# Lightning attention and a leaky-ReLU block: halves of the features, attention output on chip, compact state, weight combinations on GpSimd, TensorE in text order

## The chip, the cores and the metric

One core of a Trainium2 chip; the sets of runs used different chips. The metric is the device time of one execution in microseconds, as the median of the timed runs. A profiled execution gives the span (first to last instruction), 1.7 to 1.8 us less than its timed figure. Words used below: a *hole* is time in which TensorE waits; a *bank* is one buffer of the kernel's PSUM pool, into which its matmuls write, and tiles with the same tag share banks; a *clean* duration is that of an instruction that no other engine's work lengthens, for VectorE the mean of those that no GpSimd work overlaps; *blocking* is what VectorE's instructions took beyond that, a measured excess and not a mechanism.

## The reference, cut to what matters

```python
# q, k, v: (4, 8, 768, 64); lam: 8 decays near 0.98; blocks of 64 positions
intra = einsum('bhic,bhjc->bhij', qb, kb) * Dmask          # decayed, causal
out   = einsum('bhij,bhjd->bhid', intra, vb) + einsum('bhid,bhde->bhie', qb * lam_pow, kv_state)
kv_state = lam_block * kv_state + einsum('bhsd,bhse->bhde', kb * rev_pow, vb)
# x = out as 3072 tokens x 512
h = x @ w_in                       # 512 -> 2048, weights arrive as float64
y = maximum(0.01 * h, h) @ w_out   # 2048 -> 512
```

## The kernel before

Attention runs in chunks of 128 tokens (24 chunks, 25 pipelined *steps*: step s transposes chunk s and finishes chunk s-1). The two matrix products run in 12 *groups* of 256 tokens, each as seven products of combined quarters instead of eight (*up* to 2048 features in two calls, then one *down*). The combinations of quarters are tensor additions on VectorE. The float64 weights are turned into float32 on chip: 32 *blocks*, four VectorE operations each, then three subtractions for every pair of blocks.

```python
# weights, after the four conversion operations of a block
def t13(): nc.vector.tensor_tensor(w[:, 4:6, :], w[:, i + 1:i + 3, :], w[:, i:i + 2, :], op=ALU.subtract)
def t2():  nc.vector.tensor_tensor(at(s["T2"]), at(s["B22"]), at(s["T1"]), op=ALU.subtract)
def t4():  nc.vector.tensor_tensor(at(s["T4"]), at(s["B21"]), at(s["T2"]), op=ALU.subtract)

# one step, in text order (a = chunk to transpose, b = the chunk before it)
ps = scores of b (two PSUM banks, tag "ps")        # 64 rows, paired
sc = ps * decay                                    # VectorE, "the masks"
load(a + 2); kT[a] = transposed(k, bank "pt")      # TensorE, copied out by ScalarE
po  = state[b-1] x qsT[b]                          # state 128x128, half of it zeros
qT[a] = transposed(q, bank "pt"); qsT = qT * pow_q # GpSimd
pu  = k[b] x v[b] (tag "ps"); state = lam * state + pu   # GpSimd, VectorE, two halves
po += sc x v; xc = copy(po); dma(xs[b] <- xc)      # the attention output goes to DRAM
# ... cut ...
attend(7); need(FO // 2); load_x(0); up(0, 0)      # load_x reads xs back
attend(5); need(FO); up(0, 1)
attend(11); load_x(1); need(2 * FO); down(0)
for g in range(1, NG):
    up(g, 0); attend(1); up(g, 1)
    if g + 1 < NG: load_x(g + 1)
    down(g)
```

Every engine's order is set by a scheduler that takes what is ready, the earlier in the text first. It works before the run; in the traces of the change, e1 and e13, which share their start, every engine runs the start's instructions in the same order.

## Time and profile before

| | before |
|---|---|
| median of the timed runs | 776.83 us (773.8 to 777.11; 776.74 with a fourth run) |
| span of the profiled run | 773.9 us |
| TensorE busy | 729.7 us (94%) |
| VectorE, ScalarE, GpSimd busy | 299.8, 198.4, 73.2 us |
| moved by DMA | 55.33 MB |
| last weight conversion ends | 209.7 us |
| down of group 0 ends | 225.6 us |

The 94% tells little here: the share is an average over a start of about 220 us, in which TensorE has holes, and a long full part in which it has none.

### The profile page before, as it was taken

What the parts mean: (1) busy time and instruction counts of PE and PEld (TensorE: products, weight loads), DVE (VectorE), ACT (ScalarE), POOL (GpSimd) and SP (SyncE); (2) the same over time, 40 slices, a digit from 0 to 9 for tenths busy, and PEclk for the clock granted to TensorE, in tenths of its full rate; (3) what the DMA queues carried; (4) which work ended last, traced back from release to release, by engine and by line L of the source; (5) the groups of instructions that cost most, each with busy time, mean ns of one, the idle gap of its engine ahead of it and who ended that gap; (6) DMA issues with size and microseconds to landing.
All of it is one profiled execution on the core that took longest, in us unless ns stands there. A gap on an engine that the chain in (4) does not pass through costs nothing.

```text
span 773.9 us, 12415 instructions
## 1 busy us (share of the span) xinstructions
PE 729.7 (94%) x5312; PEld 672.6 (87%) x5312; DVE 299.8 (39%) x530; ACT 198.4 (26%) x353; POOL 73.2 (9%) x81
## 2 busy tenths in 40 slices
PE   4587999888999999999999999999999999999998
PEld 3476988777899899899998999989999899998997
DVE  6965799986613223023141230412303223032130
ACT  3423735433213022031130311302213022131220
POOL 2333141624300000000000000000000000000000
PEclk9889999999999999999999999999999999999999
DMA  9979795976400001000000000000000000000000
GB/s 227 268 183 260 193 258 130 225 190 158 118 28 19 24 28 42 14 15 28 28 29 14 15 28 28 26 3 28 28 28 2 28 28 28 28 1 28 28 1 28
DMA packets 96198, 55.33 MB, mean 71 GB/s; under 512 B 76688, under 2 KB 84880, under 8 KB 96144
## 3 DMA queue, kind: packets, MB, share of 16 engines
q1 hardware_dynamic: 96000, 54.54, 26.5%
q8 instruction: 42, 0.69, 0.4%
q14 instruction: 12, 0.10, 0.0%
q10 hardware_dynamic: 144, 0.00, 0.0%
HBM read 41.95 MB, written 12.58 MB: 70 GB/s over the span
## 4 chain that ended last, share of the span: by engine, by line
PE 83%; DVE 10%; issue 3%; ACT 2%; POOL 1%; DMA 1%; SPq 0%; ACTq 0%; DVEq 0%; POOLq 0%
PE Z L426 21%; PE Z L407 20%; PE W L426 11%; PE W L407 10%; PE Y L426 5%; PE Y L407 5%; PE ps L283 3%; PE pt L270 2%; PE po L326 2%; PE pu L310 2%; PE po L299 2%; DVE sc L287 1%; DVE wo L202 1%; DVE wo L206 1%; DVE state L319 1%
## 5 line engine op out<-in xcount | busy, mean ns | idle before, releaser
L407 PE MATMUL Z<-x,wi 128*128 128x128 f32 x1536 | 186.7, 275 | 1.0 <-ACT tmp L363 1.0
L407 PEld LDWEIGHTS Z<-x,wi 128*128 128x128 f32 x1536 | 179.5, 192 | 2.4 <-ACT tmp L363 1.2
L407 PE MATMUL W<-x,wi 128*128 128x128 f32 x768 | 93.9, 275 | 0.0
L407 PEld LDWEIGHTS W<-x,wi 128*128 128x128 f32 x768 | 89.8, 192 | 0.0
L426 PE MATMUL Z<-wo,gA 128*128 128x256 f32 x384 | 88.0, 380 | 0.0
L426 PE MATMUL W<-wo,gS 128*128 128x256 f32 x384 | 87.2, 379 | 0.0
L426 PE MATMUL Z<-wo,gS 128*128 128x256 f32 x384 | 86.9, 379 | 0.0
L426 PEld LDWEIGHTS W<-wo,gS 128*128 128x128 f32 x384 | 72.9, 190 | 10.0 <-issue 0.2
L426 PEld LDWEIGHTS Z<-wo,gS 128*128 128x128 f32 x384 | 72.8, 190 | 9.8
L426 PEld LDWEIGHTS Z<-wo,gA 128*128 128x128 f32 x384 | 71.6, 190 | 9.4 <-DVE wo L206 0.2
L363 ACT COPY tmp<-Z 128x512 f32<-128x512 f32 (+1 forms) x72 | 37.0, 514 | 156.2 <-PE Z L426 108.5
L395 ACT ACTIVATE gA<-gA 128x512 f32<-128x512 f32 x72 | 45.4, 630 | 111.9 <-DVE gA L372 45.3
L383 DVE TENSOR_TENSOR gA<-tmp,Z 128x512 f32<-128x512 f32 x24 | 16.5, 687 | 103.2 <-PE Z L407 103.2
L383 DVE TENSOR_TENSOR os<-tmp,Z 128x256 f32<-128x256 f32 x12 | 5.1, 421 | 114.2 <-PE Z L426 114.2
L372 DVE TENSOR_TENSOR gA<-tmp,Y 128x512 f32<-128x512 f32 x24 | 16.5, 688 | 80.3 <-PE Y L407 80.2
L407 PE MATMUL Y<-x,wi 128*128 128x128 f32 x384 | 47.5, 276 | 0.0
L407 PEld LDWEIGHTS Y<-x,wi 128*128 128x128 f32 x384 | 45.2, 192 | 0.4 <-issue 0.2
L283 PE MATMUL ps<-qT,kT 64*128 64x128 f32 x384 | 37.8, 300 | 7.7 <-ACT qT L272 4.6
L426 PE MATMUL Y<-wo,gA 128*128 128x256 f32 x192 | 44.4, 379 | 0.0
L283 PEld LDWEIGHTS ps<-qT,kT 64*128 64x128 f32 x384 | 31.5, 198 | 14.3 <-ACT qT L272 7.1
L426 PEld LDWEIGHTS Y<-wo,gA 128*128 128x128 f32 x192 | 36.2, 190 | 4.8
L287 DVE TENSOR_TENSOR sc<-ps,decay 128x512 f32<-128x512 f32 x48 | 31.2, 686 | 22.2 <-PE ps L283 11.2
(66 smaller groups left out, 645.1 us busy)
## 6 DMA issues: line engine op xcount, KB each, us to landing
k<-in_k_dram SPq DMA_DIRECT2D x24, 256.0 KB, 4.8
q<-in_q_dram SPq DMA_DIRECT2D x24, 256.0 KB, 5.4
v<-in_v_dram SPq DMA_DIRECT2D x24, 256.0 KB, 5.8
ws<-in_moe_w_in_dram SPq DMA_DIRECT2D x12, 512.0 KB, 5.3
xs<-xc SPq DMA_DIRECT2D x24, 256.0 KB, 2.6
x<-xs SPq DMA_DIRECT2D x24, 256.0 KB, 2.9
out_dram<-os SPq DMA_DIRECT2D x24, 256.0 KB, 2.0
ws<-in_moe_w_out_dram SPq DMA_DIRECT2D x9, 512.0 KB, 4.0
```

The costliest lines, as they stand in the source:

```text
L270: nc.tensor.transpose(out=pt[:, hp, :], in_=pair(src, hp), identity=ident)
L283: nc.tensor.matmul(ps[hi][:, hp, :], lhsT=kT[b][HALF[hi], hp, :], rhs=qT[b][HALF[hi], hp, :], start=(hp == 0), stop=True, skip_group_check ...
L287: nc.vector.tensor_tensor(sc[:, hi], ps[hi], decay[:, hi], op=ALU.mult)
L299: nc.tensor.matmul(po[:, hp, :], lhsT=state[(b - 1) % 2][:, hp, :], rhs=qsT[b][:, hp, :], start=(hp == 0), stop=False, skip_group_check=True)
L310: nc.tensor.matmul(pu[:, hp, :], lhsT=pair(loaded[b][0], hp), rhs=pair(loaded[b][2], hp), start=(hp == 0), stop=True, skip_group_check=True)
L326: nc.tensor.matmul(po[HALF[hi], hp, :], lhsT=tv[:, 2 * hp + hi, :], rhs=sc[:, hi, hp, :], start=(not inter and hp == 0), stop=True, skip_g ...
L363: nc.scalar.copy(t[:, 0:cols], src)
L372: nc.vector.tensor_tensor(c11[0], s1, Y, op=ALU.add)
L383: nc.vector.tensor_tensor(c22[0], p5, Z, op=ALU.add)
L395: nc.scalar.activation(out=dst, in_=src, func=AF.Prelu, bias=0.0, scale=1.0, alpha=0.01)
L407: nc.tensor.matmul(t[:, i * C:(i + 1) * C], lhsT=w[:, kk, :], rhs=x[:, A[sa], kk, :], start=(first and i == 0 and kk == 0), stop=(i == UP ...
L426: nc.tensor.matmul(t, lhsT=G[g][sa][:, p, :], rhs=WO[p][:, SO[sb], :], start=(first and p == 0), stop=(p == NP - 1), skip_group_check=True)
```

## The change

Its intent is to reach the full part sooner. Only 13 of the 25 steps run before group 1; the other 12 are put between an up and a down of groups 1 to 6. Up and down are done by halves of the 2048 features, so the first half can start with half of the weights. The attention output stays in SBUF. The state keeps only its two useful halves. The subtractions of weights go to GpSimd. And TensorE's order is taken from the text. The core of the diff:

```diff
+    ctx.enter_context(tc.manual_schedule(engines={mybir.EngineType.PE}))
-    state = [const.tile([P, HP, P], F32, name=f"state{i}") for i in range(2)]
+    state = [const.tile([P, HP, D], F32, name=f"state{i}") for i in range(2)]
-                nc.vector.tensor_tensor(w[:, 4:6, :], w[:, i + 1:i + 3, :], w[:, i:i + 2, :], op=ALU.subtract)
+                nc.gpsimd.tensor_tensor(W[p][:, 4:6, :], W[p][:, i + 1:i + 3, :], W[p][:, i:i + 2, :], op=ALU.subtract)
 # ... T2 and T4 likewise; cut ...
+                load(a + 1)                       # was a + 2; q has 2 buffers instead of 3
-            qT[a] = transposed(loaded[a][1], "qT")
+            qT[a] = transposed(loaded[a][1], "qT", "ps", 2)
-            xc = xp.tile([P, KO * C], F32, name="xc", tag="xc")
-            nc.sync.dma_start(out=xs[b // 2, b % 2], in_=xc)
+            nc.scalar.copy(out=X[g][:, 2 * h:2 * h + 2].rearrange("p a k c -> p (a k) c"), in_=po)
 # ... state read and update as 64-wide tiles; product() adds the first half's result; cut ...
-    W_RATE = 0.7
+    W_RATE = 0.85
+    attend(5); need(NW // 4);     up(0, 0)
+    attend(3); need(NW // 2);     down(0, 0)
+    attend(3); need(3 * NW // 4); up(0, 1)
+    attend(2); need(NW);          down(0, 1)
     for g in range(1, NG):
+        for u in range(NU):
+            up(g, u)
+            attend(1)
+            down(g, u)
```

## The prediction

The old kernel's trace: item 1 is about VectorE's conversions, item 2 about a two-input elementwise operation on GpSimd (the scaling of k and of q), item 3 about matmuls (scores that start in pairs 7 ns apart, and the next start after a change of tile shape). The forecast's sum, 765 us of span and 768 us timed, is whole: the 14 us of blocking in it rest on 0.34 us per us of GpSimd, from that trace. That the rate would hold in the changed kernel was the author's estimate. So were the pairing of 64x64 tiles, the 0.06 us of a pair of 64 columns (about half of the 112 ns measured for 128 columns) and the factor 0.93 for overlapping instructions (two masks of 0.69 us each took 1.29 us together).

> **What bounds the kernel now.** I read the page's 40 slices first, then a table of windows, the chain of waits, the groups by shape, and single steps in the timeline.
>
> ```profile
> PE   4587999888999999999999999999999999999998
> ...
> DVE  6965799986613223023141230412303223032130
> ...
> DMA  9979795976400001000000000000000000000000
> ```
>
> There are two kernels in one. From slice 11 on (about 220 us) TensorE is full and everything else idles. Before that VectorE and the DMA engines are full and TensorE has holes. The windows put numbers on it (columns: stretch, length, busy time and count on PE, PEld, DVE, ACT, POOL, granted clock, DMA share, GB/s):
>
> ```profile
> 0.00:50.00 50.00, 28.58 (x207) 23.88 (x208) 38.35 (x78) 19.00 (x32) 14.88 (x23) 0.86 0.95 231
> 50.00:79.00 29.00, 23.27 (x243) 19.43 (x242) 14.04 (x27) 8.05 (x15) 10.34 (x11) 1.00 0.96 237
> 79.00:130.00 51.00, 48.34 (x426) 44.31 (x428) 47.14 (x86) 30.41 (x53) 12.60 (x13) 1.00 0.79 197
> 130.00:202.00 72.00, 61.49 (x573) 52.97 (x570) 58.59 (x94) 25.75 (x45) 32.57 (x32) 0.98 0.74 186
> ...
> 303.60:352.80 49.20, 49.20 (x338) 46.31 (x337) 12.08 (x21) 9.98 (x18) 0.00 (x0) 1.00 0.06 22
> ```
>
> The last line is one whole group of 256 tokens in the steady part: 49.2 us, all TensorE. Instruction starts are 112 ns apart in the up products and 216 ns in the down products, so 14 x 16 x 0.112 + 7 x 16 x 0.216 = 49.3. Twelve groups are 590 us and none of the change alters them. An attention step, from the same start-to-start intervals: scores 16 x 0.056 = 0.9 (two row halves start 7 ns apart, so a pair costs 112), transposes 8 x 0.11 = 0.9, state read 8 x 0.112 = 0.9, state update 0.9, output 16 x 0.055 = 0.9, and about 0.1 at each change of tile mode: 4.8 us. With 24 chunks, four of them without the state read and four without the update, that is 108 us. 590 + 108 = 698, so about 76 of 773.9 us is TensorE waiting or running slow, nearly all of it before 227 us, when group 1 begins. That is all the change can win.
>
> [...]
> 1. [...] The conversion's last step takes 685 ns where no GpSimd work overlaps it and 1094 ns where some does; the score mask, with one input in PSUM, keeps 685 either way. From 80 to 200 us GpSimd worked 43 us and the conversions cost 14.5 us more than their clean durations: 0.34 us of VectorE lost per us of GpSimd.
> 2. [...] The trace: 1127 and 1304 ns against 687 on VectorE for 128x512.
> 3. [...] The trace shows the paired starts and 202 to 205 ns instead of 112 at each change.
>
> **The change, part by part.**
>
> *Compact state.* The state read becomes 16 instructions of 64x64. If the diagonal tiles pair as the row halves do, it stays 8 x 0.112 = 0.9 us. The update becomes 16 instructions of 64 columns, 8 pairs at perhaps 0.06: 0.5 instead of 0.9. VectorE does one 0.42 us operation instead of two, GpSimd one 0.62 instead of two. A step falls to about 4.4 us of TensorE: 20 x 0.4 = 8 us, floor 690.
>
> *Output kept on chip.* 6.3 MB written and 6.3 MB read back go away. Together with fewer chunks up front, this lowers what the start must load: 14 chunks and all weights, 11.0 + 16.8 = 27.8 MB instead of 42.7 MB in the first 210 us.
>
> *Halves, and steps spread out.* Before, 23 of 25 steps ran before the first down; now 13, and 12 run inside groups 1 to 6. Only 13 x 4.4 + 49 = 106 us of TensorE work stands before group 1, so a long start becomes shorter, and the moved steps return later at full price: 12 x 4.4, about 52 us less the 6 that two late steps cost already.
>
> *Weight combinations to GpSimd.* 16 x (683 + 417 + 416) = 24 us of clean VectorE time leaves; GpSimd gains 16 x (1.27 + 2 x 0.62) = 40 us, of which 0.34 x 40 = 14 us comes back as VectorE blocking. Net gain about 10 us.
>
> *The new start, S.* Stage A, five steps and eight weight blocks: DMA-bound. The old kernel had moved six chunks and twelve blocks by 50 us at 95% DMA share; the new one needs six chunks and about as many blocks, since its stages load ahead: 48 us. The rest up to group 1: TensorE needs 8 steps and group 0. A step has its own latency, visible in the old kernel when VectorE was half idle:
>
> ```profile
> 59.80 1.29 DVE L287 TENSOR_TENSOR sc<-ps,decay 128x512 f32<-128x512 f32 x2 [3.58 <-PE po L326]
> ...
> 65.80 1.29 DVE L287 TENSOR_TENSOR sc<-ps,decay 128x512 f32<-128x512 f32 x2 [1.17 <-PE po L326]
> ...
> 71.19 1.29 DVE L287 TENSOR_TENSOR sc<-ps,decay 128x512 f32<-128x512 f32 x2 [2.56 <-PE po L326]
> ```
>
> That is 5.4 to 6 us from mask to mask. 8 x 6.2 + 49 = 99 us by that chain. VectorE over the same stretch: 24 blocks x 2.21 = 53, 8 masks and states 14, up adds and combinations 11, down adds 1: 79 clean, times 0.93 because consecutive starts overlap, 74; GpSimd works 30 on weights and 24 on steps, x 0.34 = 18; 92 plus 5% holes = 97, then the last half down of 12: 109. The two chains overlap imperfectly. S = 48 + 106 = 154, against 227.
>
> *Steady part.* Eleven groups x 49.2 = 541. In text order a step between up and down must wait for its masks, and VectorE first finishes the combination of the up just ended. The old kernel shows this very order (the 12 matmuls of another product fill TensorE here):
>
> ```profile
> 286.60 1.16 PE L283 MATMUL ps<-qT,kT 64*128 64x128 f32 x16
> ...
> 287.33 0.69 DVE L342 TENSOR_TENSOR gS<-gS,gA 128x512 f32<-128x512 f32 x1 [1.73 <-ACT gS L395]
> ...
> 288.06 0.69 DVE L343 TENSOR_TENSOR gS<-gS,gA 128x512 f32<-128x512 f32 x1
> ...
> 288.67 0.68 DVE L344 TENSOR_TENSOR gS<-gA,gS 128x512 f32<-128x512 f32 x1
> 288.69 1.50 PE L407 MATMUL Z<-x,wi 128*128 128x128 f32 x12
> 289.27 0.69 DVE L345 TENSOR_TENSOR gS<-gA,gS 128x512 f32<-128x512 f32 x1
> 289.87 1.28 DVE L287 TENSOR_TENSOR sc<-ps,decay 128x512 f32<-128x512 f32 x2
> ```
>
> Masks end 3.9 and 4.6 us after the scores begin. The q transposes and the state update now use the two score banks, so they follow at 4.0 and 4.65, the output at 5.3, and the step ends at 6.3 instead of 4.4. Nothing may fill the hole. If the masks go first, 4.5. I take 5.4 as the middle: 12 x 5.4 = 65, where a full stall gives 75 and none 54. In the second half down, VectorE adds the first half's result to the first product; in groups 7 to 11, with no step between, it follows the four combinations, free at 3.8 us where the third product wants the bank at 3.46: 5 x 0.4 = 2. Tail 3.4 as now.
>
> Sum: 154 + 541 + 65 + 2 + 3.4 = 765; the timed runs are about 2.5 above the span (776.83 against 773.9), so 768 us, 1.1% less than before. Of 73 us taken from the start, some 59 come back as steps inside the groups, nearly a fifth of them as holes.
>
> **Rivals.**
> - *The holes outweigh the start.* Every late step stalls in full (75), and GpSimd, 60 to 80% busy in the start, slows VectorE by 0.5 instead of 0.34: S = 163, total 787, over 1% slower. For it: the order shown above, and strict order takes away what fills holes today. Against: VectorE's busy digits are 2 to 3 in the steady part.
> - *No stalls and a tight start.* Masks are served before combinations (54) and S = 142, close to what 109 us of transfers (the packets' own time on 16 engines, 55 for 14 chunks and 54 for weights) and TensorE's 106 allow: 745, 4% faster. For it: the new rates and split points look tuned, and DMA stalls behind the store and reload vanish.
> - *The transfer was hidden anyway.* After 80 us the DMA share is 0.74 to 0.79, so the roundtrip matters only in stage A, where just 0.5 MB of it moved by 50 us. Keeping x on chip alone would then gain almost nothing; the gain is in which steps come early.
> - *64x64 tiles do not pair.* The state read costs 1.8 instead of 0.9: 20 x 0.9 = 18 us more, 786.
>
> **Range and chances.** S has a spread of about 8 us, the late steps of 8, pairing and the rest of 5: together some 12. The tuned look of the split points draws the low side out. 769, with 749 to 788 for 8 in 10. Faster by over 2% means under 761.3: 0.33. Slower means over 792.4: 0.06. Within: 0.61.
>
> **What would show it.** Group 1 begins near 154 us; a half up and half down keep 25 us together; a late step takes 4.5 (no stall) or 6.3 (stall), with the q transposes waiting for the mask; VectorE 95% busy from 50 to 140 us; conversions that overlap GpSimd over 1 us; the 64x64 pairs 7 ns apart. A start beyond 165, state reads at 1.8 us, or new holes in each half down would prove me wrong upwards; a start under 140 or masks served at once, downwards.

## The result, and the profile after

The changed kernel is correct and slower: 795.78 us median (795.26 to 799.42) against 776.74, ratio 1.0264, 95% interval 1.0224 to 1.0303. Ratios here are the mean time of one kernel's fast runs over that of the other's in the same rounds, so they are not quite the ratio of the medians quoted. The prediction was 769 with 749 to 788: the kernel is slower than the whole range.

The page of the changed kernel, for the slices shown before:

```profile
PE   5287879898999999998999999989999999999998
...
DVE  6969998623313323223143043132242322423223
...
POOL 3554677301101000001011010000000000000000
PEclk9688999999999999999999999999999999999999
DMA  9955766401021022011021000000000000000000
```

Both of the old saturated resources let go earlier: VectorE after slice 7 (the last conversion ends at 155.1 us) instead of slice 10 (209.7 us). The start did become shorter. TensorE's row hardly shows what was lost in return: an 8 in slices 9, 18 and 26 (counted from 0) among nines, because 9 stands for anything from 90% up, and 20 us in 624 are 3%. The windows (columns as in the prediction; cut at the first up, the last weight conversion, the end of group 0 and the last matmul):

```profile
0.00:53.40 53.40, 27.97 (x280) 22.91 (x280) 43.33 (x70) 19.48 (x33) 25.58 (x31) 0.81 0.97 251
53.40:155.10 101.70, 82.44 (x815) 72.21 (x814) 90.33 (x132) 50.29 (x88) 56.72 (x51) 0.92 0.60 153
166.30:790.50 624.20, 603.66 (x4489) 557.49 (x4487) 182.79 (x338) 129.78 (x232) 29.80 (x27) 0.99 0.08 21
```

The full part is 624.2 us long and TensorE's busy time is 20.5 us less. Who it waited for, from the view of waits (TensorE's rows: total us, times, longest), first in the full part alone (166.3 us to the end), then in the whole run:

```profile
PE pt L253 <- DVE sc L270: 17.5, 11, 3.1
PE po L311 <- DVE sc L270: 2.0, 2, 1.8
PE Z L416 <- DVE tmp L342: 1.1, 5, 0.2
```

```profile
PE pt L253 <- DVE sc L270: 35.2, 18, 5.5
PE pt L253 <- DMA k<-in_k_dram: 12.7, 2, 7.6
PE ps L266 <- DVE state L304: 5.6, 1, 5.6
PE ps L266 <- ACT qT L255: 4.4, 2, 3.6
PE po L277 <- POOL qsT L291: 2.1, 1, 2.1
```

In the full part 19.5 of 20.6 us are waits for a mask (L270), nearly all by the transposes of q (L253). The other half of the 35.2 us, and the waits for k, the state, qT and qsT, lie in the start. The timeline of one late step shows how:

```profile
212.05 1.16 PE L266 MATMUL ps<-qT,kT 64*128 64x128 f32 x16
...
212.78 0.69 DVE L327 TENSOR_TENSOR gS<-gS,gA 128x512 f32<-128x512 f32 x1 [0.27 <-ACT gS L376]
...
214.16 0.66 PE L253 MATMUL pt<-ident,k 128*128 128x128 f32 x4
214.72 0.68 DVE L330 TENSOR_TENSOR gS<-gA,gS 128x512 f32<-128x512 f32 x1
...
215.32 1.28 DVE L270 TENSOR_TENSOR sc<-ps,decay 128x512 f32<-128x512 f32 x2
216.06 0.66 PE L253 MATMUL pt<-ident,q 128*128 128x128 f32 x4 [1.24 <-DVE sc L270]
```

The scores are there at 213.2, but the masks start at 215.32, after the four combinations of the up just ended (L327 to L330). The q transposes want the bank that the first mask reads (the change gave them tag "ps"), and in text order nothing else may run. From up to down this step takes 6.10 us. Steps that begin a batch have no state read to fill the time; their hole is longer, and then this happens:

```profile
180.97 1.55 DVE L329 TENSOR_TENSOR gS<-gA,gS 128x512 f32<-128x512 f32 x1
...
183.77 1.12 PE L253 MATMUL pt<-ident,q 128*128 128x128 f32 x4 [3.13 <-DVE sc L270]
```

Four transposes took 1.12 instead of 0.66 us: after a hole of 3.13 us TensorE ran at half clock. The windows show the granted clock (0.50, third figure from the end), here and once more after the last late step, where the hole before was 1.83 us and the first product of the half down took 3.40 us:

```profile
183.45:186.86 3.41, 3.09 (x32) 2.76 (x34) 1.29 (x3) 0.59 (x1) 1.22 (x1) 0.50 0.22 52
528.20:531.60 3.40, 3.40 (x13) 2.51 (x10) 0.00 (x0) 0.59 (x1) 0.00 (x0) 0.50 0.03 5
```

Whether a hole of some length decides it is not shown. (L329 took 1.55 us while GpSimd was scaling k beside it, and 0.68 us where no GpSimd work overlapped it.) The two steps of this kind take 8.36 and 8.46 us. In e3 (below) the first of them had the same hole and kept its full clock:

```profile
179.98 0.66 PE L253 MATMUL pt<-ident,q 128*128 128x128 f32 x4 [3.12 <-DVE sc L270]
```

That step took 7.01 us. So the longer hole costs 0.9 us over the usual 6.10, and the half clock some 1.4 more.

From the starts of the matmuls, stage by stage, the sum of the prediction against the run:

| term | predicted, us | measured, us |
|---|---|---|
| start, until group 1 begins | 154 | 166.3 |
| twelve late steps | 65 | 77.1 |
| groups 1 to 11 | 541 + 2 | 547.1 |
| tail (3.8 in the old kernel, counted alike) | 3.4 | 3.8 |
| span | 765 | 794.3 |

### The profile page after: what moved, and what is told of

Same layout as the page of the kernel before. It is cut to its first block, busy times and chain, and to the rows that moved or that the text cites. A ratio compares the mean times of both kernels' runs of the same rounds, so it can differ in the third digit from the quotient of the medians.

```text
span 794.3 us, 12974 instructions
## 1 busy us (share of the span) xinstructions
PE 725.6 (91%) x5632; PEld 662.5 (83%) x5632; DVE 319.4 (40%) x546; ACT 199.5 (25%) x353; POOL 114.8 (14%) x111
## 4 chain that ended last, share of the span: by engine, by line
PE 76%; DVE 16%; ACT 2%; issue 2%; SPq 1%; DMA 1%; POOL 1%; DVEq 0%; ACTq 0%; POOLq 0%
PE Z L393 21%; PE Z L416 20%; PE W L393 10%; PE W L416 10%; PE Y L393 5%; PE Y L416 4%; PE po L311 2%; PE pt L253 2%; DVE sc L270 2%; DVE gS L327 2%; DVE gS L329 2%; DVE gS L328 2%; PE pu L298 2%; DVE gS L330 1%; ACT gS L376 1%
## 5 line engine op out<-in xcount | busy, mean ns | idle before, releaser
L393 PE MATMUL Z<-x,wi 128*128 128x128 f32 x1152 | 140.6, 275 | 0.0
L393 PEld LDWEIGHTS Z<-x,wi 128*128 128x128 f32 x1152 | 136.1, 192 | 1.5 <-issue 0.3
L416 PE MATMUL Z<-wo,gA 128*128 128x256 f32 x384 | 93.7, 388 | 0.8 <-DVE os L364 0.8
L393 PE MATMUL W<-xs,wi 128*128 128x128 f32 x768 | 93.7, 275 | 0.8 <-ACT tmp L344 0.8
L344 ACT COPY tmp<-Z 128x512 f32<-128x512 f32 (+1 forms) x72 | 37.0, 514 | 228.1 <-PE Z L393 178.6
L393 PEld LDWEIGHTS W<-xs,wi 128*128 128x128 f32 x768 | 89.6, 192 | 0.9 <-ACT tmp L344 0.9
L287 POOL TENSOR_TENSOR k<-k,decay 128x512 f32<-128x512 f32 x20 | 25.3, 1263 | 259.1 <-PE pt L253 252.0
L253 PE MATMUL pt<-ident,q 128*128 128x128 f32 x96 | 18.6, 326 | 35.4 <-DVE sc L270 35.2
L393 PE MATMUL Z<-xs,wi 128*128 128x128 f32 x384 | 46.8, 275 | 0.0
L253 PEld LDWEIGHTS pt<-ident,q 128*128 128x128 f32 x96 | 12.3, 163 | 40.7 <-DVE sc L270 39.6
L393 PEld LDWEIGHTS Z<-xs,wi 128*128 128x128 f32 x384 | 44.8, 192 | 0.0
```

The lines of the kernel that those rows point to most:

```text
L253: nc.tensor.transpose(out=pt[:, hp, :], in_=pair(src, hp), identity=ident)
L287: nc.gpsimd.tensor_tensor(kr, kr, _bc(pow_k, 3, D), op=ALU.mult)
L344: nc.scalar.copy(t[:, 0:cols], src)
L393: nc.tensor.matmul(t[:, i * C:(i + 1) * C], lhsT=w[:, kk, :], rhs=x[:, kk, :], start=(first and i == 0 and kk == 0), stop=(i == UP - 1 and ...
L416: nc.tensor.matmul(t, lhsT=G[g, u][sa][:, i * C:(i + 1) * C], rhs=WO[UP * u + i][:, SO[sb], :], start=(first and i == 0), stop=(i == UP - ...
```

## The experiments

Theory H: the late steps cost holes because their masks queue behind the combinations, and strict order keeps TensorE from filling them. Theory G: moving the weight combinations to GpSimd was a loss. Rivals: a late step simply costs what its matmuls cost; VectorE needed the relief; the loads come too late. All kernels gave correct results. "Before" was rerun beside each set; its medians there were 775.57, 774.72, 774.72 and 776.69 us.

| run | base and edit | median us | ratio to before | interval |
|---|---|---|---|---|
| the change | | 795.78 | 1.0264 | 1.0224 to 1.0303 |
| e1_step_late | changed; step behind the half down | 773.55 | 0.9974 | 0.9951 to 0.9996 |
| e2_mask_first | changed; masks before two combinations | 776.61 | 1.0023 | 0.9995 to 1.0051 |
| e3_comb_dve | changed; weight combinations on VectorE | 790.43 | 1.0185 | 1.0156 to 1.0213 |
| e4_free_pe | changed; TensorE free | 770.23 | 0.9930 | 0.9906 to 0.9954 |
| e5_load2 | changed; loads two chunks ahead | 795.41 | 1.0258 | 1.0226 to 1.0290 |
| e6_late_comb | e1 and e3 | 767.50 | 0.9898 | 0.9871 to 0.9924 |
| e7_free_comb | e3 and e4 | 759.61 | 0.9797 | 0.9771 to 0.9822 |
| e8_old_text | before; TensorE in text order | 785.97 | 1.0137 | 1.0107 to 1.0166 |
| e9_old_comb_pool | before; weight combinations on GpSimd | 790.81 | 1.0205 | 1.0162 to 1.0249 |
| e10_x_dram | e7; attention output through DRAM | 761.90 | 0.9824 | 0.9796 to 0.9852 |
| e11_free_late | e7 and e1 | 752.84 | 0.9712 | 0.9690 to 0.9733 |
| e12_free_load2 | e7 and e5 | 758.14 | 0.9782 | 0.9758 to 0.9805 |
| e13_text_start | changed; text order in the start alone | 779.09 | 1.0026 | 0.9986 to 1.0066 |
| e14_text_groups | changed; text order in groups 1 to 11 alone | 794.78 | 1.0237 | 1.0204 to 1.0271 |
| e15_best | e7, e1 and e5 | 751.93 | 0.9689 | 0.9657 to 0.9722 |

### e1: the step behind the down

```diff
             up(g, u)
-            attend(1)
             down(g, u)
+            attend(1)
```

> Changed kernel with each late attention step moved behind its half down (up, down, step instead of up, step, down), nothing else. Theory H (late steps cost holes because their masks queue on VectorE behind the up's four combinations): the masks are served at once, a late step takes 4.5 to 4.8 us of TensorE instead of 5.6 to 8.5, the twelve give 55 instead of 77 us, the span falls by about 20 us to 773 to 777. Rival P (a late step costs what its matmuls cost, order does not matter): span unchanged within 3 us. Rival D (halves: down now follows its own up at once and waits for S2): half downs show a new wait of over 1 us each and eat most of the gain.

Measured: 773.55, 22 us less than the changed kernel. The timeline of a late step in e1, with the state read, from the down's end to the next up:

```profile
220.23 1.16 PE L266 MATMUL ps<-qT,kT 64*128 64x128 f32 x16
...
221.43 1.29 DVE L270 TENSOR_TENSOR sc<-ps,decay 128x512 f32<-128x512 f32 x2 [0.66 <-PE ps L266]
...
222.84 0.60 PE L253 MATMUL pt<-ident,q 128*128 128x128 f32 x4
...
224.86 1.38 PE L393 MATMUL Z<-x,wi 128*128 128x128 f32 x10
```

VectorE sits idle until the scores are there (0.66 before the masks), the q transposes follow without a wait, and the step takes 4.63 us. The twelve together take 52.8 instead of 77.1. Of these 24.3 us the span gains 22.9 (771.4, below the 773 to 777 expected). Six half downs that add the first half's result now take 12.67 instead of 12.19 us, as predicted for groups without a step between; the slow half down after the last step (13.60 us) is gone. The start is the same (group 1 at 166.2). Theory H stands; the rival "order does not matter" falls.

### e2: the same TensorE order, masks earlier on VectorE

```diff
         product(... quarter("A22"), 1.76)
+        if g:
+            attend(1)        # and no longer called between up and down
         combine(nc.vector, at)
```

> Changed kernel, TensorE order the same, but in VectorE's order the two masks stand before the last two of the four combinations. Theory H: the masks end about 1.3 us earlier, so each late step is 1.2 to 1.4 us shorter (6.1 to 4.8), twelve steps 15 us, and the two that fell to half clock (8.4) lose most of their excess; span about 776 to 780. Rival P: unchanged.

Measured: 776.61, 19 us less. The scheduler set the masks behind two of the four combinations, and up and step together take 17.50 instead of 18.70 us; the two long ones shrink from about 21.0 to 17.5. The twelve steps take 57.9 instead of 77.1 us, and the waits of the q transposes for a mask in the full part fall from 17.5 to 2.1 us. TensorE's order is the same as before, and the state addition still follows all four combinations on VectorE, so the place of the masks is shown to be the cause. That a q transpose waits for a mask at all is put down to the shared bank; giving it a bank of its own was not run.

### e3: weight combinations back on VectorE

```diff
-                nc.gpsimd.tensor_tensor(W[p][:, 4:6, :], ...)   # and T2, T4
+                nc.vector.tensor_tensor(W[p][:, 4:6, :], ...)
```

> Changed kernel with the weight combinations back on VectorE. Theory G (GpSimd's 51 us of combinations [...] stand before the steps' own GpSimd work, so the move was a loss at the start): group 1 begins 3 to 8 us earlier than 166.3. Rival V (VectorE is the bound of the start and 24 us off it helped): group 1 begins 8 to 15 us later. The rest of the kernel unchanged within 2 us in either case.

(GpSimd: the runs show only that VectorE's instructions took longer beside it, by the amounts below.)

Measured: 790.43, and group 1 begins at 162.5 instead of 166.3. Theory G holds at the small end of its range. How sure is that, with one profile each? The change, e1, e2 and e13 run one and the same program up to group 1, and begin it at 166.3, 166.2, 167.0 and 170.5 us: the start varies by 4 us from one execution to the next. The two runs in text order with the subtractions on VectorE, e3 and e6, begin it at 162.5 and 160.3, before all of these, and no timed run of e3 (at most 790.99) reaches one of the change (at least 795.26). The groups by shape of the changed kernel give the price on GpSimd (last numbers: busy us, mean ns, idle before):

```profile
L208 POOL TENSOR_TENSOR wi<-wi 128x512 f32<-128x512 f32 x8 | 11.9, 1488 | 17.5 <-DVE wi L197 17.5
L209 POOL TENSOR_TENSOR wi<-wi 128x256 f32<-128x256 f32 x8 | 7.1, 884 | 0.5
L210 POOL TENSOR_TENSOR wi<-wi 128x256 f32<-128x256 f32 x8 | 6.6, 828 | 0.5
```

With both halves of the weights that is 51 us of GpSimd work, for 24 us of clean VectorE time (28.9 as they ran in e3). Up to 160 us the conversions cost 29.0 us more than their clean durations (421, 420, 685, 685 ns) in the changed kernel and 9.5 in e3. The sums that combine the inputs and the ups' results (L327 to L330) took 4.6 us more than in e3 as well: up to 160 us in the changed kernel, those of 128x256 took 0.83 to 1.38 us beside GpSimd work and 0.41 without. Against the 28.9 us that left VectorE, 24.1 came back as longer instructions (sums of durations; consecutive instructions overlap a little, two masks of 0.68 us took 1.28 together, so busy time is less). Its busy time shows that nothing was left of the gain (this is e3; the changed kernel's line is the second of its windows above):

```profile
53.60:151.60 98.00, 82.87 (x816) 72.70 (x814) 89.09 (x164) 50.34 (x88) 20.87 (x18) 0.93 0.64 159
```

VectorE is busy 89.1 us there with the subtractions and 90.3 in the changed kernel without them; from the start to the last conversion it is 131.7 against 133.7. GpSimd's queue did further harm: at 42 us, for one, the scaling of q for the next step stood behind three weight subtractions in GpSimd's queue and TensorE waited 2.1 us for it.

### e4: TensorE free

```diff
-    ctx.enter_context(tc.manual_schedule(engines={mybir.EngineType.PE}))
```

> Changed kernel with TensorE scheduled freely again instead of in text order. Theory T (strict text order is what leaves the holes; the old kernel filled them with another product): the late steps' holes get filled, 12 to 20 us, and the start shortens by some us: 770 to 780. Rival S (the free order places steps and products worse or gains nothing because no other work is ready): same or slower than 794.

Measured: 770.23, 26 us less than the change (span 768.5, a little under the range given). The timeline of a late step in e4:

```profile
234.31 0.68 DVE L328 TENSOR_TENSOR gS<-gA,gS 128x512 f32<-128x512 f32 x1
...
234.85 1.03 PE L415 MATMUL Z<-wo,gA 128*128 128x256 f32 x4
...
235.52 1.28 DVE L269 TENSOR_TENSOR sc<-ps,decay 128x512 f32<-128x512 f32 x2
236.26 0.66 PE L252 MATMUL pt<-ident,q 128*128 128x128 f32 x4 [0.38 <-DVE sc L269]
```

VectorE's order is still combinations first, but four matmuls of the next down fill TensorE, and 0.38 us of hole is left.

### e5: loads two chunks ahead

```diff
-            if a:
-                load(a + 1)
             ...
             qT[a] = transposed(loaded[a][1], "qT", "ps", 2)
+            load(a + 2)
```

> Changed kernel with q, k and v asked for two chunks ahead again, as in the old one, instead of one. Theory L (the start is 12 us longer than predicted because TensorE waits 12.7 us for k in the first 50 us): the first half up begins 5 to 10 us before 53.4 and group 1 about 5 to 8 us before 166.3. Rival V (the start is set by VectorE and by the DMA total, not by the order of loads): the wait for k moves or shrinks but group 1 begins within 3 us of 166.3.

Measured: 795.41, no change. The wait for k fell from 12.7 to 6.4 us, the first up began at 53.95 and group 1 at 166.9. Other waits took its place (the state additions 5.6 to 6.8, the scaled q 2.1 to 6.8 us). Asking one chunk earlier does not move the start; the 97% DMA share up to 53.4 us speaks for the amount, but no run changed the amount.

### e6 and e7: two repairs at a time

No new edits: e6 is e1 with e3, e7 is e4 with e3.

> Both repairs in text order: late steps behind the half down and the weight combinations on VectorE. If the two costs are separate, gains add: 794 - 22 - 5 = about 767. If they share a cause (VectorE's order), about 771, no better than the step move alone.

> TensorE scheduled freely and the weight combinations on VectorE. If the GpSimd cost sits in the start whatever TensorE's order, 768.5 - 5 = about 763. If the free order already hid it, 768 as with the free order alone.

Measured: 767.50 and 759.61. In e6 the gains add (22 and 5 of 28). In e7 taking the combinations off GpSimd is worth 10.6 us instead of the expected 5: TensorE in the free order still waited for GpSimd's weights in e4 (2.3 us for one product alone), and not in e7. e7 is the first version some 2% below the old kernel (its interval, 0.9771 to 0.9822, leaves open whether it is more or less); e4 and e6 lie below it by 0.7 and 1%.

### e8: the old kernel in text order

The same line as in e4, added to the old kernel.

> The old kernel with TensorE in text order, nothing else. Theory T (strict order costs by itself, because other products no longer fill the waits of the start): 10 to 30 us slower than 774, nearly all of it before group 1 begins at 227. Rival (the order matters only where steps lie inside groups, and the old kernel has two such): within 5 us of before.

Measured: 785.97, 11 us slower than before; but hardly before group 1. Group 0's down ends at 226.9 (225.6 before). The rest comes after: in the old kernel group 1's down ends only 48.4 us later, because 40 of the 56 matmuls of the step in it and 18 of its 224 up matmuls (from 206.8 us on) had been done in the holes of group 0; in e8 it ends 55.5 us later, with a step of 6.13 in the middle, and the last step takes 6.41. So the amount was as expected and its place was not.

### e9: the old kernel with weight combinations on GpSimd

```diff
-                nc.vector.tensor_tensor(w[:, 4:6, :], ...)   # and T2, T4
+                nc.gpsimd.tensor_tensor(w[:, 4:6, :], ...)
```

> The old kernel with the weight combinations on GpSimd, nothing else. If the net of the changed kernel holds (24 us of clean VectorE time removed, about 19 us returned as blocking, GpSimd's queue longer for the steps), the old kernel is 0 to 5 us slower. If the prediction's sum held (net gain 10 us of VectorE time at a start that VectorE bounds), it is 5 to 10 us faster.

Measured: 790.81, 16 us slower than before, more than any branch expected. The last conversion ends at 228.8 instead of 209.7 us. (This profile is of the slowest run, 795.54.) The conversions' excess over their clean durations grew from 12.1 to 16.7 us between 80 and 200 us, while GpSimd's work grew from 43.3 to 69.1: too little to explain it. VectorE's waits grew beside it: from 79 us to the last conversion it waited 15.8 us for scores (11.2 before), 7.3 for ScalarE's part of a conversion (1.2) and 8.9 for the state update (3.5). By which route GpSimd's longer queue brings this about in the old order was not isolated.

### e10: the attention output through DRAM

```diff
-            nc.scalar.copy(out=X[g][...], in_=po)
+            xc = xp.tile([P, KO * C], F32, name="xc", tag="xc")
+            nc.scalar.copy(out=xc, in_=po.rearrange("p a b -> p (a b)"))
+            nc.sync.dma_start(out=xd[g, h], in_=xc)
+            if h == 1:       # X[g] is read back in two transfers; NX = 5 to make room
```

> The best version so far (changed kernel, TensorE scheduled freely, weight combinations on VectorE; 759.6 us) with the attention output written to DRAM and read back as in the old kernel, five x buffers instead of six to make room. If the roundtrip was hidden anyway: within 2 us. If it held up the start (about 20 us of packets on all 16 engines in the first 160 us): 4 to 10 us slower.

Measured: 761.90 against 759.61 for its base, 2.3 us, just outside "hidden". The two come from different sets, and their intervals against the old kernel overlap. The last conversion is 4.7 us later (153.2 against 148.6), of which 2.3 reach the total. The buffer count changed with it, so the roundtrip alone is not measured: some 2 us is all that it can be seen to cost.

### e11 and e12: the best version with one more repair

> The best version so far with the late steps behind the half down. If the free order already fills every hole with other products, within 2 us of 759.6; if holes of some tenths per step are left, 3 to 8 us faster.

> The best version so far with q, k and v asked for two chunks ahead. The wait for k (9 us in that run) should shrink; if the first 50 us are bound by what the DMA engines move and not by order, within 2 us of 759.6; else 3 to 6 us faster.

Measured: 752.84 and 758.14. Moving the step is worth 6.8 us even in the free order, at the upper end: the filling in e4 was not complete. The earlier loads change 1.5 us, within the 2 us of "no effect" and with overlapping intervals; no gain is shown.

### e13 and e14: strict order in one part alone

The same statement as a block around the start (e13) or around the loop over groups (e14).

> Changed kernel, TensorE in text order only up to the end of group 0, free afterwards. If the strict order hurts only the late steps (holes of 1.5 us and more that a free order fills): 772 or less, close to the 770 of the fully free order. If it hurts mostly the start: 782 to 790.

> Changed kernel, TensorE free up to the end of group 0, in text order in groups 1 to 11. If the strict order hurts only the late steps: about 794, like the changed kernel. If the start owns a part, 794 less that part; the two parts of e13 and e14 should add up to the 26 us of the free order, within 4.

Measured: 779.09 and 794.78. Against the change, freeing the groups alone won 16.7 us and freeing the start alone 1.0; together 17.7, not the 26 of e4, so the expected addition failed. Part of the gap is the start's spread: e13's profiled run began group 1 at 170.5 us, 4.2 later than the change with the same program. Counted from the end of group 0 to the last matmul, the change takes 624 us, e14 621, e13 605 and e4 596: 3 and 19 us alone, 28 together, so some 6 us come only with both. The traces say why. In e14 the last conversion ends at 156.6 and group 0 at 167.4 (155.1 and 166.3 in the change): a free TensorE does not end a start sooner that waits for weights, though its first up matmul stands at 23.9 us instead of 53.4. What it can do is begin group 1 in those waits: its first up matmul stands at 149.6 us in e4 and at 166.3 in the change. In e14 it did begin early, at 148.4, but the groups' strict order stood behind it and its down ended at 228.1, against 219.6 in e4 and 230.3 in the change. The overlap pays in full only with freedom on both sides of the border.

### e15: everything that won

> Free order, weight combinations on VectorE, late steps behind the half down, loads two chunks ahead: gains add to about 751, 3% faster than the old kernel. If the last two share their gain, 753.

Measured: 751.93, 3.1% faster than before (ratio 0.9689) and 5.5% faster than the change by the medians. It is within a microsecond of e11, so the earlier loads add nothing that these runs can show.

## Why the prediction was wrong

*What bounds the kernel, and what the change can win:* right in the main. The 76 us of waiting lay in the start, and the change did shorten it. But "227, when group 1 begins" was late: the old kernel's first up matmul of group 1 stands at 206.8 us (see e8), so the start ended less sharply than the comparison of 154 with 227 makes it look.

*Compact state:* right from the trace; it was not undone in a run. The 64x64 state read takes 1.02 us for 16 instructions (0.9 predicted), the update 0.52 (0.5), a step without a hole 4.63 (4.5). In the state read the two tiles of a pair start 6 to 7 ns apart and the pairs 109 to 110 ns, so the rival in which tiles do not pair falls.

*Output kept on chip:* its worth was left open and the third rival called it nearly hidden; e10 shows no more than 2.3 us.

*Weight combinations to GpSimd, "Net gain about 10 us":* this step failed: nothing was gained. The rate of 0.34 us lost per us of GpSimd came out again for the conversions alone (29.0 us over 85.0 us of GpSimd work up to 160 us). What failed is the quantity it was applied to and what it left out: the subtractions took 51 us on GpSimd instead of 40, the combinations of inputs and results were blocked too (4.6 us), and GpSimd's queue delayed the steps. VectorE stayed as busy as in e3, 133.7 against 131.7 us. Undoing it gained 5 to 6 us in text order (e3, e6) and 10.6 in the free order (e7).

*The start, "S = 48 + 106 = 154":* the term was mis-sized by 12.3 us. The prediction's own sign of being wrong upwards, a start beyond 165, came true. The first part took 53.4 instead of 48. Then VectorE was busy 90.3 us where 92 were predicted, but idle 11.4 where 5 were: 101.7 instead of 97. Group 1 followed 11.2 us after the last conversion (12 predicted). So VectorE's chain, which gave 109, was the right one, and shading it to 106 towards TensorE's chain was an error of 3. Of the 12.3, e3 and e6 tie 4 to 6 to GpSimd; e5 and e14 show that neither loads one chunk earlier nor TensorE's order is the rest. The cause of the remaining 6 to 8 us stays open; the start's own spread of 4 us may be part of it, and what would shorten the first 53 us was not found.

*The steady part, "I take 5.4 as the middle":* this is the second step that failed, and it was a choice, not an argument. The working gave masks ending 3.9 and 4.6 us after the scores (measured 3.95 and 4.55), a step of 6.3 (6.10) and 75 us for twelve (77.1). The trace of the old kernel had already shown the order; there was nothing to average. Three stretches at half clock, some 1.4 us each (two in steps, one in the half down after the last), were not foreseen.

*The groups:* 547.1 instead of 543. The wait of a second half down was right (0.48 us in five groups, 0.4 predicted). The rest is about 0.1 us at each change of stage around a step and the one half down of 13.60 us, at half clock in its first 3.4 us.

*Slips in the prediction's figures*, none of which decides: the 2.5 us between timed and span mix two executions (the profiled one was timed at 775.64, so 1.7); the 14.5 us behind the rate hold 2.4 us on the subtractions, and the conversions alone lost 12.1; the chain of steps uses 6.2 us a step where its lines show 5.4 to 6.0; VectorE was not full all the way to 220 us (14.0 of 29.0 us in the second window); the 1094 ns are a mean of ten, from 677 to 1665.

*The rivals and the chances:* the first rival, "the holes outweigh the start" with 787, is the nearest to what happened: every late step stalled in full and S was 166 (163 there), though for its reason, 0.5 us lost per us of GpSimd, the runs show 0.34. Being slower was given 0.06, and the look of the split points ("tuned") drew the range down, which is no evidence from the profile. And one effect of strict order has no term in the sum: it also forbids group 1 to begin in the holes of group 0. e4, e13 and e14 show it to be worth some 6 us on top of what each freedom wins alone.

## What to carry to other kernels

Strict order on the bound engine turned the late answers of a helper engine into holes here (19.5 us of waits for a mask in the full part); before fixing it, put each dependent piece where its helpers are idle (here behind the down: 22 us from moving one line), or leave the order free. When the helper's order is already visible in the old trace, take the time it gives and do not average it with a hope. Moving work to GpSimd beside a saturated VectorE returned nothing here (28.9 us of instructions off, 24.1 us back as longer ones, the same busy time), and work queued behind it waited (TensorE 2.1 us for a scaled q). And where the same program begins a stage 4 us earlier or later from run to run, one profile does not settle a difference of that size.

## What the traces show of the hardware

- VectorE beside GpSimd: the conversions on VectorE lost 0.34 us for each us of GpSimd work in the changed kernel (29.0 over 85.0 us up to 160 us), 0.28 in the old one (12.1 over 43.3 us, 80 to 200 us) and 0.24 in e9 (16.7 over 69.1 us): the rate differed from program to program. The masks, with one input in PSUM, took 673 to 692 ns in the changed kernel, beside GpSimd work or not. GpSimd's instructions were longer in the busy start as well: a 128x256 subtraction took 724 ns at best and 907 and 851 on average, and the scaling of q 1461 ns on average up to 160 us against 1272 in the full part.
- GpSimd against VectorE, two-input subtractions: the best cases took 1.86 times VectorE's clean time for 512 elements and 1.74 for 256 (1267 against 683, 724 against 416 ns); on average in the busy start GpSimd took 2.0 to 2.2 times it (1434, 907 and 851 against 683, 417 and 416).
- The clock of TensorE: holes of 3.13 us (twice) and of 1.83 us were followed by 3.4 us at half clock in the changed kernel; one of 3.12 us in e3 was not, and those of 1.24 us never were.
- A change of tile shape: in the old kernel the next instruction starts 202 to 205 instead of 112 ns later.
